# A sparse-softmax attention and low-rank mixer kernel: a planner's order of tasks and PSUM banks replaced by a written-out list, and sixteen loads moved from GpSimd's queue to SyncE's

## The chip, the cores and the metric

The kernel runs on one NeuronCore of one Trainium2 chip. A core has five engines that take their instructions in program order and wait for each other by semaphores: TensorE (PE, matmul and transpose), VectorE (DVE), ScalarE (ACT), GpSimd (POOL) and SyncE (SP, which here only issues DMAs). PE writes into PSUM, which has eight banks of 128 x 512 fp32. The metric is the device time of one launch in microseconds. Before the change four runs gave 603.37, 605.27, 605.30 and 608.26, with a median of 605.28.

## The reference, cut to what matters

```python
batch, n_heads, seq, head_dim = (8, 8, 576, 64)      # tau = 0.02
def _attn_ref(q, k, v, tau):
    scores = (1.0 / np.sqrt(64)) * np.matmul(q, k.transpose(0, 1, 3, 2))
    thresh = np.max(scores, axis=-1, keepdims=True) - tau
    scores = np.where(scores >= thresh, scores, -1000000000.0)
    scores = scores - np.max(scores, axis=-1, keepdims=True)
    attn = np.exp(scores)
    attn = attn / (np.sum(attn, axis=-1, keepdims=True) + 1e-09)
    return np.matmul(attn, v).astype(np.float32)
def _moe_ref(x, U, V, w_ch1, w_ch2):                 # x: heads side by side, (8, 576, 512)
    h = x.transpose(0, 2, 1) @ U @ V                 # rank 32 over the sequence
    u = x + h.transpose(0, 2, 1)
    ch = np.maximum(u @ w_ch1, 0.0) @ w_ch2          # 512 -> 2048 -> 512
    return (u + ch).astype(np.float32)
```

## The kernel before

Two heads form a head pair; there are four pairs in a batch and 32 in all, numbered from 0. A pair has 576 rows, cut into four tiles of 128 and one of 64; the 64-row tiles of two pairs are computed together, so that two pairs need nine score steps, and the whole kernel has 144.

The work of a pair is cut into tasks, each a short Python function that emits a few instructions for one engine. In the order of the data they are: load_tasks (eight DMAs for q and k, L458, and three for v, L480), turn_main and turn_rest (PE transposes q and k, L518 and L531; ACT copies them to SBUF), high, low4 and low (v split into two bf16 halves, ACT L546 and POOL L553), scores (PE, L587, fp32, 16 short matmuls for each step), weigh (DVE, L616, scales the scores and takes the row maximum while it moves them out of PSUM), threshold and exponential (ACT, L632 and L639), select (DVE, L646, keeps what passes the threshold and sums it), twin (POOL, L664, copies a 64-column remainder), turn_w (SP, L670, a DMA that transposes the weights) or turn_pe (PE, L677, the same by TensorE, used for some tiles of the first eight pairs), product (PE, weights times v, L746 to L754), low_part, join and norm (ACT, DVE, POOL: division by the sum), narrow, low_rank, copy_tt, spread and sum_u (the low-rank part), and narrow_u with send_u or turn_u (the transpose of u). A batch then has sixteen up tasks (PE, L930, each four matmuls of 128 x 512), four rest tasks in every second batch (L946), ACT's relu (L920), four or five groups of four down tasks (PE, L963), finish (DVE, L975) and send (SP, L986 and L987). The up and down tasks are the only large blocks of PE work that no later task of the attention waits for.

Every weigh needs its scores in PSUM. A scores task for two steps uses the six banks of the two trio tiles; a task for one step uses four of them. All other PE tasks take one bank each, from those that are free at that time.

The tasks are made in a plain order, and class Order decides in what order they are emitted. Its run is a list scheduler: for each engine it keeps the tasks whose inputs are ready, estimates when each could start from costs written at the tasks, and takes the one with the lowest rank, which is the time at which it became ready plus an offset from the table OFF (one number for each kind of task and phase). The up and down tasks are ranked by DUE and a count of score steps instead. The bank of a task is chosen at the same time. When the estimate leaves PE idle for more than 0.45 us, run emits fillers, which are matmuls of the identity into a free bank (L421, fill) that keep PE busy and whose result nobody reads. What run emits is a fixed program: on the chip each engine executes its list in order.

In the first pairs the queue of an engine matters: a DMA is issued by an engine as an instruction in its list. Pair 0's q and k are loaded by SP, ACT and POOL; those of all later pairs by POOL (variables eq, ek and e3 in load_tasks), v by SP. The mixer's weights are loaded by POOL (weight_loads, L1003 to L1026), spread over the first 30 score steps.

Of the kernel before, what the change touches and what calls it, by code (L numbers as in the profile page):

```python
# [68 lines left out]
P = 128  # L69
# [18 lines left out]
LONE = 2  # L88

# [4 lines left out]
DUE = (461, 86.25, 1468.5, 516.25, 1049.25, 748, 134.75, 1357.5)  # L94
# [32 lines left out]

class Order:


    SIGNAL = (0.25, 0.08, 0.08, 0.08, 0.1)
    LAG = (0.0, 0.07, 0.1, 0.06, 0.0)
    SLOW = (1.0,) * 5
    TO_PE = 0.15
    SELF = 0.07
    WARM = 7.2
    BEFORE = 0.45
    PATIENCE = (0, 0.2, 0.1, 0.9, 1.35)


    BEGIN = (3.34, 4.5, 0.7, 1.3, 0.7)
    LANES = 8
    SHARE = (0.6, 0.4)
    LANDING = (3.1, 1.4)
    SWITCH = {"quadrants": 0.17, None: 0.13}
    PARTS = {"S": "quadrants"}

    HOLD = (61.76, 61.61, 6.12, 44, 94.32, 94.08, 76.76, 0.01, 9.57)
    KEPT = ((), (0, 1, 3, 4), (0, 1, 2, 3, 4, 5))


    OFF = {
        "copy_main": (25.53, 63.74, -194.99, 34.77, -69.14, 17.14, -324, 37.67, -35.45),
        "copy_rest": (6.5, -40.06, -14.53, 24.12, -4.13, -20.91, -46.23, 54.32, -95.65),
        "copy_tt": (-16.03, -64.1, 20.85, -110.66, 55.87, 62.18, -42.53, -53.37, -25.08),
        "copy_u": (89.47, -53.33, 162.09, -74.19, 7.13, 9.51, -102.11, -20.31, -73.82),
        "copy_u4": (-5.3, -56.82, -16.18, -6.54, 49.93, -37.52, 64.79, -22.2, -18.99),
        "copy_w": (75.7, -4.79, -22.58, 20.52, -4.75, 68.84, -1.46, 27.15, 10.06),
        "down": (52.39, 32.35, 33.69, 38.82, 7.25, -27.49, 1.69, 19.34, 131.97),
        "exponential": (61.02, 15.66, 97.71, -26.58, 23.56, 95.43, 116.8, 90.08, 11.21),  # L160
        "finish": (-53.17, -45.71, 51.42, 30.79, -14.22, -26.29, 28.78, 16.33, -75.01),
        "first": (-56.79, 75.89, 0.92, -55.7, 35.86, -3.48, 9.68, 53.63, 1.2),
        "high": (-129.72, -35.78, 31.87, -6.58, 48.08, -20.33, -28.95, -46.46, 84.01),
        "inverse": (46.71, -32.89, 54.08, 22.1, 122.91, 38.13, 143.23, 39.39, -23.27),
        "join": (2.19, 36.38, 69.81, -65.72, -28.72, -7.68, -26.75, 24.75, -3.5),
        "load": (14.89, -38.6, -1.87, -55.09, 439, 169.52, 202.43, 266.17, -64.61),
        "low": (23.82, 3.88, -45.02, 6.6, -28.12, -60.17, -87.19, -43.1, 26.46),
        "low4": (64.5, 130.96, 545.14, -26.82, 13.94, -59.21, 35.95, 265.72, -23.85),
        "low_part": (30.38, 13.98, -26.01, -41.71, 130.31, 109.34, -20.82, -133.07, -1.88),
        "low_rank": (-57.69, 16.1, -2.98, 31.4, -60.74, 41.37, 38.61, 8.08, -35.05),  # L170
        "make": (-18.31, -192.85, -81.78, -52.29, 6.69, -18.25, 12.16, -35.09, 27.21),
        "narrow": (5.95, 39.32, -9.64, -6.72, 1.46, 29.45, -10.31, 45.69, -47.12),
        "narrow_u": (-45.99, -94.08, -136.7, -16.38, -46.01, -113.33, 15.29, 42.82, -0.02),
        "narrow_u4": (2.02, -41.08, 15.16, 12.95, 69.79, 35.67, -44.1, -54.14, 56.42),
        "norm": (60.22, 26.73, 14.75, 16.35, 28.89, -20.28, -16.45, 55.02, 19.4),
        "product": (-38.14, -97.33, -17.17, 18.14, -78.98, 56.88, 40.12, 68.18, -110.66),
        "relu": (44.72, -2.34, -31.3, -83.46, 20.06, -116.77, 10.32, 4.5, -36.91),
        "rest": (64.49, 74.43, 34.29, 18.04, -20.78, -41.41, -55.22, -17.62, 44.45),
        "scores": (-2.16, -56.15, 42.01, -69.96, -15.23, -44.76, 4.79, -16.69, -3.93),
        "select": (-41.99, 29.22, -2.51, 135.03, 570.07, 400.28, 184.53, 231.57, 188.34),  # L180
        "send": (43.87, 17.75, 5.67, -19.7, -14.51, -9.84, 285.3, 70.92, -48.56),
        "send_u": (54.83, -57.33, -16.36, 177.37, 12.48, 121.89, 19.74, 60.45, 25.84),
        "spread": (-216.88, 63.66, -12.54, -9.53, -23.32, -1.29, -122.3, 43.34, 63.38),
        "spread4": (12.62, -19.59, -18, 54.22, -34.85, 61.33, -24.98, -50.63, -66.91),
        "spread_v": (-113.69, -64.83, 6.03, 44.27, 73.51, -47.79, -27.38, 65.24, 2.79),
        "sum_u": (-64.77, 3.32, 13.18, 117.53, -78.44, -9.21, 87.33, 127.21, -64.36),
        "sum_u4": (-96.51, 65.77, 2.32, 38.3, 44.64, 21.12, -125.78, 37.98, 23.47),
        "sums": (195.64, 23.57, 47.14, -31.56, 10.32, -16.1, 35.4, 4.49, -58.98),
        "threshold": (-37.94, -91.24, -43.1, -296.86, 94.89, 36.19, 66.3, 1.07, 12.5),
        "turn4": (-36.19, -43.45, 5.14, 7.01, 54.44, -61.28, 52.57, 29.57, -92.54),  # L190
        "turn_main": (0.34, 20.57, 26.79, -161.06, 126.25, -30.36, -38.23, -14.86, -5.97),
        "turn_pe": (-0.48, -21.65, -184.33, 36.36, -95.83, 51.55, 181.65, 20.16, -43.63),
        "turn_rest": (-5.99, -37.64, -0.75, 52.43, -6.2, -61.13, -8.69, -94.49, -32.06),
        "turn_u": (-85.8, -3, -69.47, -45.79, 74.76, -7.02, 3.37, 12.83, 72.77),
        "turn_w": (45.6, -1.19, -137.3, 47.86, -48.09, 10.25, -28.07, -30.73, 72.41),
        "twin": (32.78, -132.71, -13.72, -15.07, -38.22, -14.87, -64, 49.79, 55.76),
        "up": (13.07, 75.42, -49.49, -57.58, 68.34, -48.43, 10.3, 58.82, 35),
        "values": (-37.57, -25.94, -48.38, 20.3, -54.04, 26.74, 72.56, -4.07, -32.49),
        "weigh": (-145.66, -20.29, -57.18, 79.45, -16.94, 55.31, 45.2, 33.27, 31.94),
        "weights": (-56.28, 79.24, -10.97, 18.21, -35.76, 31.57, -73.46, 67.52, 113.68),  # L200
    }
# [4 lines left out]
    def add(self, *args, **kw):  # L206
        t = Task(*args, **kw)
        t.phase = self.phase
        t.lag = 0.0 if t.dma else self.LAG[t.engine]
        t.off = self.OFF[t.fn.__name__][self.phase]  # L210
        self.tasks.append(t)
        return t

    def run(self):
        ready = [[] for _ in range(5)]
        for t in self.tasks:
            t.left = len(t.deps)
            for d in t.deps:
                d.after.append(t)
            if not t.left:  # L220
                ready[t.engine].append(t)
        at = list(self.BEGIN)
        last = [0.0] * self.nbanks
        kind = None
        steps = 0
        locked = 0.0

        moved = [0.0, 0.0]

        lanes = [0.0] * self.LANES  # L230

        def rank(c):
            s, t = c
            if t.when is not None:
                due = t.when <= steps + (1.0 if t.kind == kind else 0.0)
                return (t.when - 1000.0 if due else t.when + 1000000.0, s)
            return (t.ready + t.off, s)

        left = len(self.tasks)
        while left:  # L240
            best = None
            free = sorted(range(self.nbanks), key=lambda n: last[n])
            kept = self.KEPT[max([t.trios for t in ready[PE] if t.ready <= at[PE] + self.HOLD[t.phase]],
                                 default=0)]
            pool = [n for n in range(self.nbanks) if n not in kept]
            soonest = min(last[n] for n in pool)
            for e in range(5):
                cands = []
                for t in ready[e]:
                    s = max(at[e], t.ready)  # L250
                    if t.banks:
                        s = max(s, soonest)
                    if t.trios:
                        s = max([s] + [last[n] - self.BEFORE * (t.steps == 1)
                                       for n in self.KEPT[t.trios]])
                    if e == POOL and t.dma:
                        s = max(s, lanes[t.ndma - 1 - self.LANES])
                    if s < NEVER:
                        cands.append((s, t))
                if not cands:  # L260
                    continue
                first = min(s for s, _ in cands)
                s, t = min((c for c in cands if c[0] <= first + self.PATIENCE[e]), key=rank)
                if best is None or s < best[0]:
                    best = (s, t)
# [3 lines left out]
            if e == PE:  # L269
# [7 lines left out]
                if parts != self.PARTS.get(kind):  # L277
                    s += self.SWITCH[parts]
# [820 lines left out]
```

## Time and profile before

The profiled execution took 603.37 us, which is the lowest of the four; its span, from the first instruction to the last, is 601.6 us, so that 1.77 us lie around it.

| | busy us | share of the span | instructions |
|---|---|---|---|
| PE | 584.0 | 97% | 6249 |
| DVE | 522.0 | 87% | 1399 |
| ACT | 458.8 | 76% | 959 |
| POOL | 372.1 | 62% | 596 |

The granted TensorE clock is 1.00 in nearly all of the span. The 84 fillers are counted in PE's busy time with 22.9 us. In the breakdown by DMA queue, the queue that SP issues to carries 66.3 MB in 207,680 packets and POOL's carries 22.8 MB in 14,048.

Two things should be kept in mind with this page. Busy times of neighbouring matmuls and of neighbouring vector instructions overlap, since an instruction's record runs until its last result is written; the distance from one start to the next is shorter than the record. A filler's record is 0.379 us long, for instance, but a row of fillers starts one every 0.217 us. And a filler is busy time in the table but not work.

### The profile page before, as it was taken

How to read it: one execution, taken by the hardware profiler on the slowest of the kernel's cores; microseconds unless marked ns; L12 is line 12 of the kernel's file. 1: busy time of each engine (PE TensorE's matmuls, PEld its weight loads, DVE VectorE, ACT ScalarE, POOL GpSimd, SP SyncE). 2: the span in 40 equal slices, each digit the busy share in tenths (PEclk: the TensorE clock that was granted, in tenths of full speed). 3: DMA queues.
4: the chain of work that ended last, by engine and by line, in shares of the span. 5: the costliest groups of instructions: out<-in, count | busy, mean ns of one | idle time of the engine just before them, and what ended most of it. 6: DMA issues, size and time to landing. Idle time of an engine off the chain costs nothing. (4 is left out here: it accounts for less than half of the span.)

```text
span 601.6 us, 17115 instructions
## 1 busy us (share of the span) xinstructions
PE 584.0 (97%) x6249; PEld 349.3 (58%) x6249; DVE 522.0 (87%) x1399; ACT 458.8 (76%) x959; POOL 372.1 (62%) x596
## 2 busy tenths in 40 slices
PE   7999889999999999999999999999999999999996
PEld 3455665666666556555665556555566666556642
DVE  4889999999999999999988999999999999994101
ACT  5757899998899866896789866897699986784540
POOL 9958587687888864576676665776677633342000
PEclk9999999999999999999999999999999999999999
DMA  7799989958999799988998899887999987667203
GB/s 161 112 179 154 169 138 172 167 115 139 206 181 165 135 187 197 172 152 140 196 167 147 147 189 180 164 161 158 188 165 150 177 156 147 124 95 131 45 1 87
DMA packets 222771, 90.48 MB, mean 150 GB/s; under 512 B 200800, under 2 KB 213040, under 8 KB 222688
## 3 DMA queue, kind: packets, MB, share of 16 engines
q1 hardware_dynamic: 207680, 66.30, 65.7%
q0 software_dynamic: 14048, 22.76, 20.6%
q8 instruction: 49, 0.80, 0.6%
q10 hardware_dynamic: 960, 0.34, 0.2%
q14 instruction: 34, 0.28, 0.2%
HBM read 37.90 MB, written 9.44 MB: 79 GB/s over the span
## 5 line engine op out<-in xcount | busy, mean ns | idle before, releaser
L639 ACT ACTIVATE e_sb<-s_sb,m 128x576 bf16<-128x576 f32 x288 | 217.7, 775 | 42.8 <-DVE s_sb L616 33.0
L646 DVE SCALAR_TENSOR_TENSOR w_ring<-s_sb,thr,e_sb 128x576 bf16<-128x576 f32 x288 | 238.7, 858 | 8.8 <-ACT e_sb L639 3.9
L616 DVE TENSOR_SCALAR_CACHE_REDUCE s_sb<-trio 128x576 f32<-128x576 f32 x288 | 203.2, 751 | 16.1 <-PE trio L587 14.9
L587 PE MATMUL trio<-qkT 64*64 64x288 f32 (+2 forms) x2304 | 162.9, 410 | 0.5 <-DVE x L791 0.4
L664 POOL COPY w_ring<-w_ring 128x128 bf16<-128x128 bf16 (+1 forms) x168 | 72.5, 442 | 103.7 <-DVE w_ring L646 82.4
L587 PEld LDWEIGHTS trio<-qkT 64*64 64x64 f32 x2304 | 83.6, 132 | 56.9 <-issue 10.9
L458 POOL DMA_DIRECT2D qkraw<-in_q_dram x125 | 82.3, 663 | 25.1 <-PE bank L518 20.1
L798 POOL TENSOR_TENSOR x<-x,rec 128x256 f32<-128x256 f32 (+1 forms) x84 | 69.5, 830 | 37.4 <-DVE x L791 29.0
L963 PE MATMUL bank<-W2b,R 128*128 128x512 bf16 x368 | 90.2, 379 | 0.4 <-ACT qkT L524 0.3
L963 PEld LDWEIGHTS <-R 128*128 128x128 bf16 x576 | 53.8, 98 | 54.1 <-issue 1.5
L458 POOL DMA_DIRECT2D qkraw<-in_k_dram x125 | 81.3, 658 | 3.0 <-issue 2.2
L930 PE MATMUL bank<-uT,W1b 128*128 128x512 bf16 x320 | 77.8, 379 | 0.7 <-ACT R L920 0.4
L930 PEld LDWEIGHTS <-W1b 128*128 128x128 bf16 x512 | 47.1, 98 | 53.6 <-issue 5.7
L553 POOL TENSOR_TENSOR vh<-vraw_ring,vh 64x128 bf16<-64x128 f32 x64 | 56.1, 877 | 13.8 <-ACT vh L546 8.1
L750 PEld LDWEIGHTS <-wT_ring 128*128 128x128 bf16 x896 | 56.0, 98 | 7.6 <-issue 2.6
L920 ACT ACTIVATE R<-bank 128x512 bf16<-128x512 f32 x91 | 52.7, 595 | 4.8 <-PE bank L930 3.0
L930 PE MATMUL trio<-uT,W1b 128*128 128x512 bf16 x192 | 48.3, 379 | 0.4 <-DVE s_sb L616 0.2
L963 PE MATMUL trio<-W2b,R 128*128 128x512 bf16 x208 | 47.5, 379 | 0.0
L632 ACT ACTIVATE thr<-m,tau_t 128x2 f32<-128x2 f32 x144 | 42.0, 294 | 3.7 <-DVE s_sb L616 3.5
L750 PE MATMUL bank<-vh,wT_ring 128*128 128x128 bf16 x624 | 44.5, 219 | 0.0
L975 DVE TENSOR_TENSOR o<-bank,x 128x512 f32<-128x512 f32 x23 | 15.8, 688 | 32.1 <-PE bank L963 31.9
L746 PE MATMUL bank<-vh,wT_ring 128*128 128x64 bf16 x176 | 33.9, 193 | 0.0
(105 smaller groups left out, 719.7 us busy)
## 6 DMA issues: line engine op xcount, KB each, us to landing
out_dram<-o SPq DMA_DIRECT2D x71, 128.0 KB, 3.1
vraw_ring<-in_v_dram SPq DMA_DIRECT2D x32, 160.0 KB, 3.7
qkraw<-in_k_dram POOLq DMA_DIRECT2D x63, 80.0 KB, 4.4
qkraw<-in_q_dram POOLq DMA_DIRECT2D x62, 80.0 KB, 4.2
vraw_ring<-in_v_dram SPq DMA_DIRECT2D x32, 128.0 KB, 3.9
qkraw<-in_q_dram POOLq DMA_DIRECT2D x63, 64.0 KB, 3.8
qkraw<-in_k_dram POOLq DMA_DIRECT2D x62, 64.0 KB, 4.4
W1b<-in_moe_w_ch_dram POOLq DMA_DIRECT2D x8, 256.0 KB, 6.1
```

The lines of the kernel that those rows point to most:

```text
L458: queue.dma_start(pr.qkraw[part, to, j, :], src[:, j, of, :])
L553: nc.gpsimd.tensor_tensor(out=pr.vh[part, tiles_, :, h, :], in0=raw[part, tiles_], in1=pr.vh[part, tiles_, :, 0, :], op=ALU.subtract)
L587: mm = nc.tensor.matmul(cols[part, lo:hi], a.tT[hs, 0, rows], a.tT[hs, 1, lo:hi], start=True, stop=True)
L616: nc.vector.tensor_scalar(out=s_sb, in0=score_cols(slot, x), scalar1=-scale, scalar2=None, op0=ALU.mult, op1=ALU.min, accum_out=m[:, x:x + 1])
L639: nc.scalar.activation(out=e_sb, in_=s_sb, func=ACT.Exp, bias=m[:, x:x + 1], scale=-1.0)
L646: nc.vector.scalar_tensor_tensor(out=w_sb[:, 0:S], in0=s_sb, scalar=thr_[:, x:x + 1], in1=e_sb, op0=ALU.is_le, op1=ALU.mult, accum_out=pr. ...
L664: nc.gpsimd.tensor_copy(out=w_sb[:, xs, S:640], in_=w_sb[:, xs, 512:S])
L750: nc.tensor.matmul(av[:, 2 * a + j, :], w, pr.vh[:, kt, j, :, :], start=kt == 0, stop=False)
L798: nc.gpsimd.tensor_tensor(out=x, in0=x, in1=over_sum(part), op=ALU.mult)
L920: nc.scalar.activation(out=R2[:, fts, lo:hi], in_=bank[t.got[0]].rearrange("p (f c) -> p f c", c=hi - lo), func=ACT.Relu)
L930: nc.tensor.matmul(bank[t.got[0]], W1b[:, dt, ft * P:(ft + 1) * P], bt.uT[:, dt, :], start=(dt == 0), stop=(dt == 3))
L963: nc.tensor.matmul(ch, R2[:, ft, lo:lo + P], W2b[:, ft, :], start=(ft == 0), stop=(ft == 15))
```

## The change

The scheduler is removed: the tables OFF, HOLD and PATIENCE, the cost constants and the whole selection in run are gone. In its place stand two constants. ORDER lists all 3284 tasks by number in the order in which they are emitted, with negative entries for fillers (-1 - bank); BANK gives the PSUM bank of each task that needs one. The tasks themselves are made in the same order as before, so a number means the same task in both kernels. The list has 56 fillers where the scheduler had emitted 84. It changes the order on all five engines.

The q and k loads of pairs 1 and 2 (counted from 0), eight DMAs each, are issued by SP and no longer by POOL (LOADERS). Two dependencies are added: the second weigh of a two-step scores task is put behind the first (both are on DVE), and the transpose of u of every pair waits for the up tasks of the batch two before it, where only the first pair of a batch did. Some cost numbers at the tasks change, which nothing reads any more, and an unused variant (take and over, for p < ACTED with ACTED = 0) is added.

```diff
+LOADERS = (None, "SSSS", "SSSS")
+ACTED = 0
+ORDER = (
+    23, 21, 22, 25, 20, 26, 24, 19, 44, 28, 46, 40, 27, 29, 42, -1, -1, -1, -1, -1, -1, -1, -1, -1, 32, 41, 30, 33,
...
+)
+BANK = {n: b for b, tasks in {
+    0: (
...
+}.items() for n in tasks}
     def run(self):
-        ready = [[] for _ in range(5)]
...
-            s, t = best
...
+        for n in ORDER:
+            if n < 0:
+                self.filler(-1 - n)
+                continue
+            t = self.tasks[n]
+            assert all(d.end for d in t.deps), "a task before what it needs"
             if t.trios:
                 t.got = list(self.KEPT[t.trios])
             elif t.banks:
-                t.got = [min((n for n in pool if last[n] <= max(s, soonest)),
-                             key=lambda n: (n < 6, n % 3 < 2, last[n]))]
...
+                t.got = [BANK[n]]
             t.fn(t)
...
+            t.end = True
...
-        eq, ek, e3 = (POOL, POOL, POOL) if p else (SP, SCA, POOL)
+        by = {"S": SP, "A": SCA, "P": POOL}
+        eq, ek, eq3, ek3 = (SP, SCA, POOL, POOL) if p == 0 else \
+            (by[c] for c in (LOADERS[p] if p < len(LOADERS) else "PPPP"))
...
-            t = add(VEC, 0.678, weigh, [S_, got("w", tiles[0] + x - NS)],
+            t = add(VEC, 0.678, weigh, [S_, got("w", tiles[0] + x - NS)] + ([done["P1", n - 1, x]] if slot else []),
...
-        deps = [ub] + (done.get(("p1", pr.b - 2), []) if pr.hp == 0 else [])
+        deps = [ub] + done.get(("p1", pr.b - 2), [])
```

## The prediction

> **What bounds the kernel now.** I read the table of busy times first, then the busy times in six stretches (cut at 25, 50, 94, 330 and 532 us), then the same stretches for the fillers' line alone.
>
> ```profile
> PE 584.0 (97%) x6249; PEld 349.3 (58%) x6249; DVE 522.0 (87%) x1399; ACT 458.8 (76%) x959; POOL 372.1 (62%) x596
> ```
>
> ```profile
> 0.00:25.00 25.00, 21.52 (x158) 10.44 (x159) 16.09 (x50) 14.58 (x29) 23.51 (x43) 1.00 0.67 136
> 25.00:50.00 25.00, 23.36 (x320) 14.23 (x317) 20.36 (x59) 15.95 (x32) 18.47 (x36) 1.00 1.18 170
> 50.00:94.00 44.00, 38.95 (x580) 25.83 (x582) 42.23 (x119) 39.36 (x80) 30.99 (x53) 1.00 1.02 158
> 94.00:330.00 236.00, 234.58 (x2602) 144.59 (x2603) 223.68 (x604) 198.74 (x425) 169.43 (x268) 1.00 0.95 164
> 330.00:532.00 202.00, 200.90 (x2147) 119.81 (x2146) 197.33 (x525) 160.25 (x340) 121.50 (x187) 1.00 0.92 160
> 532.00:601.60 69.60, 64.66 (x453) 34.37 (x452) 22.34 (x50) 29.92 (x59) 8.24 (x13) 1.00 0.36 69
> ```
>
> ```profile
> 0.00:25.00 25.00, 10.48 (x35) 3.59 (x36) 1.00 0.67 136
> 25.00:50.00 25.00, 8.78 (x37) 3.14 (x34) 1.00 1.18 170
> 50.00:94.00 44.00, 3.29 (x13) 1.19 (x13) 1.00 1.02 158
> ```
>
> The columns are the stretch, its length, busy PE, PEld, DVE, ACT and POOL, granted clock, DMA share and GB/s; in the second fence PE and PEld are the fillers alone. From 94 us on PE is full (234.58 of 236, 200.90 of 202). Before that up and down have nothing to work on, and a good part of PE's busy time is filler. So the time is PE's own work plus what PE loses, and nearly all of the loss lies in the first 94 us, where the attention's chain and DVE set the pace.
>
> **The ledger.** From the PE timeline I take each kind of task by its usual distance from one start to the next where nothing waits, in us. 128 up and 144 down at 0.864: 235.0. 24 one-step scores at 1.133, 60 two-step at 2.102, and 0.093 for each of 84 changes into scores: 161.1. The products, 56 at 1.009, 28 at 0.505, 8 at 1.05 and 4 at 0.524: 81.1. 64 turn_main at 0.437, 32 turn_rest at 0.110: 31.5. The small ones (rest, low_rank, spread, turn_pe, turn_u, spread4, turn4): 41.8. Sum 550.5, the same in both kernels. The span of 601.6 thus has a loss of 51.1: 36.8 up to score step 25 (PE starts it at 93.9 us with 57.1 of work done), 9.0 from there to step 142 (532.0 us, 486.2 done), 5.3 after it, of which 4.7 follow the last matmul. Up to step 25 the loss is 3.3 before the first instruction, 83 fillers at 0.217 = 18.0, 1.8 because the first nine take 0.42 each, and 13.7 of waits.
>
> DVE gets the same ledger, by the same distances: weigh 0.678, select 0.738, sum_u and finish 0.603, join 0.31, make 0.29, inverse 0.335. The built programs give the order, so the work ahead of a step can be counted in both:
>
> | step | PE starts it, before | PE work ahead, before / after | fillers | DVE work ahead, before / after |
> |---|---|---|---|---|
> | 8 | 35.4 | 14.7 / 14.7 | 53 / 31 | 20.4 / 21.7 |
> | 25 | 93.9 | 57.1 / 58.8 | 83 / 56 | 76.4 / 77.2 |
> | 90 | 339.0 | 297.2 / 285.2 | 84 / 56 | 297.3 / 297.2 |
> | 142 | 532.0 | 486.2 / 479.8 | 84 / 56 | 475.5 / 475.2 |
>
> Two things follow. 27 of the 28 missing fillers are missing before step 25, 22 of them before step 8. And after step 25 the new order brings the scores forward and leaves up and down for later: 12 us at step 90, 6.4 at step 142.
>
> **The moved loads.** These rows are POOL's, SP's, PE's and DVE's timelines:
>
> ```profile
> 3.08 2.62 POOL L458 DMA_DIRECT2D qkraw<-in_q_dram  x4
> 24.78 1.38 POOL L664 COPY w_ring<-w_ring 128x128 bf16<-128x128 bf16 x7
> ```
>
> ```profile
> 3.17 4.36 SPq L480 DMA_DIRECT2D vraw_ring<-in_v_dram  x6
> 25.17 5.14 SPq L670 DMA_TRANSPOSE wT_ring<-w_ring  x3
> ```
>
> ```profile
> 29.23 3.63 PE L421 MATMUL trio<-identb 128*128 128x512 bf16 x16
> 34.80 0.41 PE L754 MATMUL bank<-vh,wT_ring 128*128 128x64 bf16 x8 [1.32 <-DMA wT_ring<-w_ring]
> ```
>
> ```profile
> 32.76 0.82 DVE L646 SCALAR_TENSOR_TENSOR w_ring<-s_sb,thr,e_sb 128x576 bf16<-128x576 f32 x1 [2.85 <-DMA wT_ring<-w_ring]
> ```
>
> Before, POOL issues loads at 0.655 each until 24.78, and the first seven twins stand behind them although DVE's first selects ended by 16 us. So SP's first transpose starts at 25.17, the first product waits behind 16 fillers, and DVE stands 2.85 us for a ring slot. In the new program four tasks of v's split and loads, one weight DMA and pair 0's loads are ahead of the first twin: v lands near 11, ACT's cast 0.7, low4 and low 1.9, two loads 1.3, a weight 0.6, twin near 16. SP has 25 DMAs ahead of its first transpose: 0.74, three in 2.38, 22 at 0.727, which gives 19.1. Transposes start 6 us earlier, and the 16 fillers at step 8 are gone from the list.
>
> What the move costs: pair 1's loads, which POOL had issued by 8.3, are now mixed with v on SP; the last starts at 10.4 and lands 3.7 later (the median of SP's q loads), at 14.1. turn_rest of pair 1 ran at 12.88 and now stands ahead of step 2 with both turn_main (0.98 together), so step 2 starts at 15.2 where it was 14.2: a loss of 1.0, taken in full. Pair 2's loads stand ahead of the first transpose in any case and are in the 19.1.
>
> The Trainium skill ("DMA: Bandwidth & Descriptors", Issuing engines are not separate DMA queues) says that spreading DMAs over issuing engines saves only the sequencer's time, usually small beside the transfer; by that the move gives about nothing. Here sixteen issues of 0.655 are 10.5 us in a queue that a transpose waits behind.
>
> **Fillers.** A filler on the list costs 0.217, one that is left out costs nothing only if the task behind it is ready. I take 27 x 0.217 = 5.9 as gained. From below the bound is 0 (PE waits instead). From above it is DVE's: weigh of step 25 cannot start before 10.3 + 77.2 = 87.5, 1.9 after its scores, so PE starts step 25 no earlier than 85.6 and loses at least 85.6 - 58.8 = 26.8, 10.0 less than now. 36.8 - 5.9 + 1.0 = 31.9 lies between.
>
> Against leaving fillers out speaks the Trainium skill ("TensorE: Matmul & The Clock Gate", Part 1): after an idle window of about 3.4 us PE falls to half clock. By it one such gap would cost some 1.7 us more. The trace shows the slow clock only in the first nine fillers (0.42 against 0.217), and no PE gap over 1.7 us after them.
>
> **Step 25 to 142.** The waits there sum to 9.0. Those over 0.15 us (nineteen, such as low_rank to up 0.60, fill to down 0.46) make 5.5, the rest is in small gaps. Most come where PE stands at one task while up or down could run; an order by single tasks can put one in between. Bounds: 3.5 (all nineteen gone) and 9.0 (none); I take the middle, 6.2.
>
> **The other edits.** Bank numbers cost nothing by themselves; a bank taken too early would show as a PE wait, in the range. The weigh dependency is between neighbours on DVE. The u dependency could hold SP, with every transpose behind it, only if up of two batches earlier is late; when batch 3 begins (steps 54 to 57) 36 up tasks are ahead, 32 are needed. The cost numbers are read by nobody.
>
> **Sum.** 550.5 + 31.9 + 6.2 + 5.3 = 593.9 of span; 1.77 around it gives 595.7 on the profiled run's footing; the median lies 1.91 above that run: 597.6.
>
> **The rivals.** That the change does nothing is excluded: the built lists differ on every engine.
>
> *Nothing gained (605 to 607).* PE waits where it filled, and the 9.0 stays: 36.8 + 9.0, with or without the 1.0. For it: fillers only mark time. Against it: the 2.85 us of DVE and the 16 fillers have one cause, POOL's queue, which is removed.
>
> *DVE becomes the bound (slower, 611).* The new order needs DVE to run ahead. From its first weigh at 10.3 to weigh of step 142 at 534.3 DVE does 475.5 in 524.0, 90.7%. If it does no better, that weigh stays at 534, its scores at 532, and PE still has 70.7 instead of 64.3 to do: 532 + 70.7 + 5.3 = 608.0, or 611.7 as a median. It decides below 475.2 / 517.6 = 91.8%, where the time is as before; my sum needs 93%. For it: from 94 to 330 us the DMA share is 0.95 and transposes must come faster too. Against it: DVE's idle time here is PE's making, since PE is full.
>
> *More gained (591).* DVE's limit is nearly reached in the start (loss 28) and the nineteen waits go: 550.5 + 28 + 3.5 + 5.3 = 587.3, median 591.0.
>
> **Numbers.** Forecast 0.50, more 0.20, nothing 0.16, slower 0.14. A measurement of this kernel tells about 0.5%, that is 3.0 us: faster is below 602.3. Forecast and more are faster: 0.70; same 0.16; slower 0.14. The forecast's own range is 593 to 602 (waits 3.5 to 9.0, the gain in fillers between 5.9 and 3, the 1.0 gone or doubled). For 8 in 10 I take 590 to 606, which leaves out slower and a little below.
>
> **What would show it.** Right: SP's first transpose near 19 us, no wait of select for wT near 30, step 25 started near 90.7, step 142 near 518, DVE at 93% between. Wrong: PE waits of several us in the first 90 us; selects waiting for transposes or weigh for scores after 94 us; a last matmul later than 594.

## The result, and the profile after

The changed kernel takes 604.83 us as a median of 53 runs (600.2 to 611.94), the kernel before 606.21 of 79 (601.34 to 610.24). The ratio is 0.9976, with an interval of 0.9961 to 0.9990. That is a gain of 0.24%, clear of the noise and below the 0.5% that the prediction set as a bound: by its classes, the same. The profiled run took 603.87 us with a span of 602.1, which is 0.5 more than the span of the kernel before; the forecast for it was 593.9.

The first view is again the table of busy times.

```profile
PE 577.9 (96%) x6221; PEld 345.5 (57%) x6221; DVE 515.3 (86%) x1399; ACT 458.3 (76%) x959; POOL 335.7 (56%) x580
```

PE has 6.1 us less busy time, about what the 28 missing fillers took (the fillers' records sum to 22.9 us before and 16.5 after), and yet the span is not shorter. The six stretches (columns as in the prediction) tell where it went:

```profile
0.00:25.00 25.00, 21.40 (x167) 10.78 (x171) 16.74 (x52) 14.05 (x27) 15.06 (x31) 1.00 0.79 155
25.00:50.00 25.00, 22.65 (x342) 14.18 (x342) 24.93 (x73) 20.70 (x43) 20.49 (x38) 1.00 1.11 158
50.00:94.00 44.00, 40.08 (x577) 26.09 (x576) 41.49 (x116) 39.85 (x82) 30.39 (x53) 1.00 1.01 155
94.00:330.00 236.00, 228.82 (x2584) 140.85 (x2582) 226.40 (x612) 196.62 (x419) 155.48 (x266) 1.00 0.96 164
330.00:532.00 202.00, 201.19 (x2144) 120.18 (x2143) 190.88 (x521) 162.85 (x346) 107.24 (x184) 1.00 0.95 157
532.00:601.60 69.60, 63.78 (x420) 33.39 (x417) 14.86 (x30) 24.18 (x49) 7.03 (x11) 0.99 0.39 76
```

From 25 to 50 us DVE is busy for 24.93 of 25 us where it was 20.36: the start is better, as forecast. From 94 to 330 us PE is busy for 228.82 of 236 us where it was 234.58: PE waits 6 us more there, in a stretch where it had been full. The ledger of the prediction, with the same work of 550.5 in both, gives the loss in three parts:

| loss in us | up to step 25 | steps 25 to 142 | behind step 142 | sum | span |
|---|---|---|---|---|---|
| before | 36.8 | 9.0 | 5.3 | 51.1 | 601.6 |
| forecast | 31.9 | 6.2 | 5.3 | 43.4 | 593.9 |
| after | 30.8 | 14.0 | 6.7 | 51.5 | 602.1 |

So 6.0 us were gained up to step 25 and 6.4 given back behind it. PE's timeline names the larger waits (in brackets the idle time before the instruction and what ended it):

```profile
109.71 0.66 PE L572 MATMUL bank<-ident,qkraw 128*128 128x128 f32 x4 [1.70 <-DVE x L859]
...
178.19 0.30 PE L585 MATMUL bank<-ident,qkraw 128*128 128x128 f32 x1 [1.31 <-DMA qkraw<-in_q_dram]
...
233.35 1.02 PE L1031 MATMUL bank<-W2b,R 128*128 128x512 bf16 x4 [1.91 <-DVE o L1043]
...
297.63 0.33 PE L585 MATMUL trio<-ident,qkraw 128*128 128x128 f32 x1 [0.69 <-DVE s_sb L670]
298.30 0.40 PE L964 MATMUL bank<-identb,ub 128*128 128x128 bf16 x4 [0.34 <-ACT ub L957]
...
579.84 1.02 PE L1031 MATMUL trio<-W2b,R 128*128 128x512 bf16 x4 [1.17 <-ACT R L988]
```

(The ledger counts 0.1 to 0.2 more for each, since it goes by the distance of starts.) In the rows of 109.71, 233.35 and 297.63 PE waits for a bank that DVE frees, and DVE's timeline shows why it was late:

```profile
107.01 0.82 DVE L700 SCALAR_TENSOR_TENSOR w_ring<-s_sb,thr,e_sb 128x576 bf16<-128x576 f32 x1 [2.12 <-DMA wT_ring<-w_ring]
...
229.88 2.69 DVE L700 SCALAR_TENSOR_TENSOR w_ring<-s_sb,thr,e_sb 128x576 bf16<-128x576 f32 x1
...
232.61 0.69 DVE L1043 TENSOR_TENSOR o<-bank,x 128x512 f32<-128x512 f32 x1
...
294.37 2.30 DVE L700 SCALAR_TENSOR_TENSOR w_ring<-s_sb,thr,e_sb 128x576 bf16<-128x576 f32 x1
```

At 107 us a select waits 2.12 for a transpose of its ring slot; two more selects and the join (L859) that frees PE's bank stand behind it. At 229.88 a select lasts 2.69 instead of 0.82, and the finish (L1043) that frees PE's bank stands behind it; at 294.37 it is 2.30. POOL's timeline beside the two:

```profile
230.22 0.62 POOL L866 TENSOR_TENSOR x<-x,rec 128x256 f32<-128x256 f32 x1
230.79 1.16 POOL L607 TENSOR_TENSOR vh<-vraw_ring,vh 128x512 bf16<-128x512 f32 x1
...
294.88 1.17 POOL L607 TENSOR_TENSOR vh<-vraw_ring,vh 128x512 bf16<-128x512 f32 x1
```

The low task of pair 13 (L607) runs from 230.79 to 231.95, right behind a norm task (L866), and the select ends 0.62 later. The same holds at 294.37, without a norm: low ends at 296.05, the select at 296.67.

The marks of the start stand as forecast, on SP and on POOL:

```profile
19.12 3.24 SPq L724 DMA_TRANSPOSE wT_ring<-w_ring  x2
```

```profile
15.35 0.30 POOL L718 COPY w_ring<-w_ring 128x128 bf16<-128x128 bf16 x1
```

SP's first transpose is issued at 19.12 (25.17 before; 19.1 forecast), the first twin runs at 15.35 (24.78 before; near 16 forecast), and no select waits for a transpose near 30 us. The later mark does not stand: PE starts step 142 at 524.6, where 518 was forecast.

### The profile page after: what moved, and what is told of

Read it like the earlier page. It is cut to its first block, busy times and chain, and to the rows that moved or that the text cites. A ratio compares the mean times of both kernels' runs of the same rounds, so it can differ in the third digit from the quotient of the medians.

```text
span 602.1 us, 16997 instructions
## 1 busy us (share of the span) xinstructions
PE 577.9 (96%) x6221; PEld 345.5 (57%) x6221; DVE 515.3 (86%) x1399; ACT 458.3 (76%) x959; POOL 335.7 (56%) x580
## 4 chain that ended last, share of the span: by engine, by line
PE 55%; DVE 19%; DMA 6%; issue 5%; ACT 5%; SPq 1%; POOL 0%; DVEq 0%; ACTq 0%; POOLq 0%
PE trio L641 13%; DVE w_ring L700 9%; PE trio L998 8%; PE bank L998 6%; PE trio L1031 6%; PE bank L1031 6%; DVE s_sb L670 6%; DMA wT_ring<-w_ring 4%; PE bank L804 4%; PE trio L804 3%; ACT e_sb L693 2%; PE bank L572 1%; DVE o L1043 1%; PE trio L572 1%; DMA qkraw<-in_q_dram 1%
## 5 line engine op out<-in xcount | busy, mean ns | idle before, releaser
L693 ACT ACTIVATE e_sb<-s_sb,m 128x576 bf16<-128x576 f32 x288 | 215.8, 774 | 39.9 <-DVE w_ring L700 27.4
L718 POOL COPY w_ring<-w_ring 128x128 bf16<-128x128 bf16 (+1 forms) x168 | 66.9, 404 | 127.3 <-DVE w_ring L700 92.3
L510 POOL DMA_DIRECT2D qkraw<-in_q_dram x117 | 76.7, 657 | 12.2 <-PE bank L572 4.9
L866 POOL TENSOR_TENSOR x<-x,rec 128x256 f32<-128x256 f32 (+1 forms) x84 | 54.9, 660 | 38.6 <-DVE x L859 25.0
L607 POOL TENSOR_TENSOR vh<-vraw_ring,vh 64x128 bf16<-64x128 f32 (+1 forms) x64 | 53.9, 842 | 23.7 <-ACT vh L600 11.1
L998 PE MATMUL trio<-uT,W1b 128*128 128x512 bf16 x272 | 65.6, 379 | 0.4 <-ACT tt L885 0.4
L998 PE MATMUL bank<-uT,W1b 128*128 128x512 bf16 x240 | 59.5, 379 | 0.0
L988 ACT ACTIVATE R<-trio 128x512 bf16<-128x512 f32 x74 | 41.8, 597 | 15.6 <-PE trio L998 13.5
L988 ACT ACTIVATE R<-bank 128x512 bf16<-128x512 f32 x70 | 40.7, 595 | 5.3 <-PE bank L1014 3.3
L804 PE MATMUL bank<-vh,wT_ring 128*128 128x128 bf16 x512 | 36.7, 219 | 0.0
L1043 DVE TENSOR_TENSOR o<-trio,x 128x512 f32<-128x512 f32 x13 | 8.9, 690 | 31.5 <-PE trio L1031 31.4
```

What stands on the lines that cost most here:

```text
L510: queue.dma_start(pr.qkraw[part, to, j, :], src[:, j, of, :])
L607: nc.gpsimd.tensor_tensor(out=pr.vh[part, tiles_, :, h, :], in0=raw[part, tiles_], in1=pr.vh[part, tiles_, :, 0, :], op=ALU.subtract)
L693: nc.scalar.activation(out=e_sb, in_=s_sb, func=ACT.Exp, bias=m[:, x:x + 1], scale=-1.0)
L718: nc.gpsimd.tensor_copy(out=w_sb[:, xs, S:640], in_=w_sb[:, xs, 512:S])
L804: nc.tensor.matmul(av[:, 2 * a + j, :], w, pr.vh[:, kt, j, :, :], start=kt == 0, stop=False)
L866: nc.gpsimd.tensor_tensor(out=x, in0=x, in1=over_sum(part), op=ALU.mult)
```

## The experiments

All ratios are to the kernel before, run on the same chip; the parts of the loss are from each kernel's profiled run. "DVE idle" is the time up to the weigh of step 142 less DVE's work ahead of it, by the prediction's ledger.

| run | ratio | interval | up to 25 | 25 to 142 | behind 142 | sum | DVE idle |
|---|---|---|---|---|---|---|---|
| before | 1 | | 36.8 | 9.0 | 5.3 | 51.1 | 58.8 |
| after | 0.9976 | 0.9961 to 0.9990 | 30.8 | 14.0 | 6.7 | 51.5 | 51.0 |
| new start, old list | 0.9878 | 0.9824 to 0.9932 | 31.2 | 8.7 | 5.1 | 45.0 | 52.9 |
| old start, new list | 1.0102 | 1.0053 to 1.0152 | 37.8 | 19.2 | 6.5 | 63.5 | 63.2 |
| loads back on POOL | 0.9969 | 0.9936 to 1.0001 | 31.1 | 16.1 | 6.6 | 53.8 | 53.5 |
| loads moved alone | 1.0013 | 0.9978 to 1.0049 | 39.9 | 8.8 | 5.2 | 53.9 | 61.7 |
| five places on PE and DVE | 0.9978 | 0.9948 to 1.0007 | 28.8 | 15.5 | 5.0 | 49.3 | 50.5 |
| two low tasks | 0.9960 | 0.9931 to 0.9988 | 30.6 | 12.5 | 6.8 | 49.9 | 49.4 |
| old list, 35 fillers fewer | 1.0042 | 1.0008 to 1.0076 | 41.0 | 9.2 | 5.2 | 55.4 | 63.1 |
| new start, 12 fillers | 0.9942 | 0.9914 to 0.9970 | 33.8 | 9.8 | 5.2 | 48.7 | 56.3 |
| old list, 25 fillers fewer | 1.0032 | 1.0003 to 1.0062 | 39.4 | 12.0 | 5.2 | 56.6 | 64.3 |
| low tasks and tail | 0.9896 | 0.9850 to 0.9941 | 29.0 | 13.5 | 4.9 | 47.4 | 48.7 |
| low, tail and v loads | 0.9859 | 0.9825 to 0.9892 | 30.6 | 7.4 | 5.0 | 43.0 | 44.3 |
| v loads alone | 0.9982 | 0.9949 to 1.0015 | 30.6 | 12.8 | 6.8 | 50.2 | 49.7 |

One caution for the column "up to 25": six kernels have the changed kernel's list and loads unchanged up to step 25, and lie between 28.8 and 30.8. A difference of 2 us in one profile of the start is no finding.

A second one concerns PE's granted clock. In every profile it is 1.00 from 6 to 10 us on, but for the last few microseconds and, in some, stretches of 3.41 or 6.83 us at 0.50. Between steps 25 and 142 there are such stretches in "old start, new list" (two, from 199.6 and from 244.0 us), "loads back on POOL" (from 112.2), "five places" (109.6), "two low tasks" (110.7) and "old list, 25 fillers fewer" (110.4), and none in the other rows. One of 3.41 us can make up 1.7 us of that column (an estimate: half its length).

**Was the gain of the start given back by the list behind it?** The first run has the new list up to score step 23 and everything else in the old order, the second the reverse (with the loads on POOL).

```diff
-ORDER, BANK = new
+ORDER, BANK = new up to the scores of step 23, then the rest in the old order
```

> The new list up to score step 23, the old order and banks for everything after it. Theory 'given back': the new list gains some 6 us of PE loss before step 25 (36.8 to 30.8 in the traces) and loses it after that by waits that belong to the later part of the list (9.0 to 14.0, and 5.3 to 7.3 behind step 142). Then the loss here is 30.8 + 9.0 + 5.3 and the span about 596, a ratio of 0.990. Rival 'elastic': whatever is gained early is lost later, because transposes and DVE cannot keep up with an earlier start in any order; then the loss between steps 25 and 142 grows to 13 or more here too and the ratio is 0.997 to 1.000.

```diff
-ORDER, BANK = new
+ORDER, BANK = old up to the scores of step 23, then the rest in the new order
-LOADERS = (None, "SSSS", "SSSS")
+LOADERS = ()
```

> The old order (loads of pairs 1 and 2 on POOL) up to score step 23, the new list and banks after it. Theory 'given back': loss 36.8 + 14.0 + 7.3, a span near 608.6, ratio 1.010. Rival 'elastic': the later part loses less when it starts later, about 9 and 5, span near 602, ratio 1.000.

The first came out at 0.9878, the second at 1.0102, near what the theory of "given back" says. In the first the losses are where it puts them, 31.2 and then 8.7. In the second they are 37.8 and then 19.2, which is 5.2 more than the theory's 14.0; the two stretches of slow clock can be 3.4 of these, and the profiled execution was the slowest of its six. The new list behind step 25 is worse than the old one after either start. The elastic rival falls, since an early start keeps its gain with the old list behind it. The first run is faster than both kernels.

**Which part of the change makes the start faster?**

```diff
-LOADERS = (None, "SSSS", "SSSS")
+LOADERS = ()
```

> The changed kernel with the q and k loads of pairs 1 and 2 back on POOL, everything else in the same list. If the move is what makes the start faster: the first twin comes again behind some 20 us of POOL's loads, SP's first transpose near 25 us, the loss at step 25 rises from 30.8 to 35 or more, ratio 1.005 to 1.010 against the kernel before. If the order does it and the move nothing: first transpose below 21 us or loss at step 25 below 32, ratio as the changed kernel's, 0.998.

```diff
-ORDER, BANK = new
+ORDER, BANK = old
 LOADERS = (None, "SSSS", "SSSS")
```

> The old order and banks, with the q and k loads of pairs 1 and 2 issued by SP: the move alone. The 83 fillers ahead of step 25 stay on the list, 18.0 us. If the move frees the start: first transpose near 19 us, DVE's 2.85 us wait at 30 us gone, loss at step 25 33 to 35 in place of 36.8, ratio 0.994 to 0.997. If a list made for late transposes cannot use it: loss 36 to 38, ratio 0.999 to 1.003.

The list does it, not the move. With the loads back on POOL the start loses 31.1; with the move alone 39.9, which is 3.1 more than before and more than either expectation said (its time can't be told from that of the kernel before). SP's first transpose in the one and in the other, POOL's first twin in the first, and a load of POOL's in the second:

```profile
17.54 4.19 SPq L664 DMA_TRANSPOSE wT_ring<-w_ring  x2
```

```profile
27.50 5.01 SPq L664 DMA_TRANSPOSE wT_ring<-w_ring  x3
```

```profile
17.19 0.32 POOL L658 COPY w_ring<-w_ring 128x128 bf16<-128x128 bf16 x1
```

```profile
16.35 2.62 POOL L450 DMA_DIRECT2D qkraw<-in_q_dram  x4 [12.13 <-PE bank L525]
```

In the new list the first twin stands behind two of the eight loads of pair 3, but ahead of the other six, of the loads of Ub and of four casts of Vb. So the transpose is early even when the sixteen loads are put back into POOL's queue, where all of them stand ahead of that twin. In the old list seven twins stand behind all eight loads of pair 3, and taking the sixteen loads out of the queue doesn't bring the twins forward: POOL stands 12.13 us at the first load of pair 3, which waits for PE to free its buffer, and the twins come at 26.65. No run moved the twins alone, so that their place is what makes the start faster is argued from these times. The move alone makes step 2 start at 17.1 instead of 14.2, since pair 1's loads wait among v's on SP.

**Are the late waits a matter of where PE's and DVE's tasks stand?**

```diff
-DVE: 666 select, 664 select, 678 select, 580 join, 695 weigh
+DVE: 580 join, 666 select, 664 select, 695 weigh, 678 select
-PE: 1288, 1284, 1286 transposes of pair 12, 1033 product, 845 rest
+PE: 1033 product, 845 rest, 1288, 1284, 1286 transposes of pair 12
-DVE: 1386 select, 867 finish
+DVE: 867 finish, 1386 select
-DVE: 1785 select, 1891 weigh, 1890 weigh
+DVE: 1890 weigh, 1785 select, 1891 weigh
-PE: 2870 down, 3250 rest, ... 2871 down, ... 3230 up, 3278 down, 2872 down, 3254 down, 3255 down
+PE: 2870 down, 2871 down, 2872 down, 3250 rest, ... 3230 up, 3254 down, 3255 down, 3278 down
```

Four bank numbers change with the order.

> The changed kernel with its list altered at five places only, where PE waited over 1.3 us after 94 us. DVE's join of pair 4 (it frees the bank that turn_main of pair 8 waits for at 109.7) ahead of two selects that wait for a transpose; a product and a rest task ahead of the transposes of pair 12, whose load lands late (178.2); finish of batch 1's third tile ahead of the select that lasted 2.69 us (233.4); a weigh ahead of the select that lasted 2.30 us (297.6); the last two downs of batch 6 ahead of batch 7's relus, and the first 64-row down behind two others (568 and 580). Fifteen tasks out of 3284 move, four banks change. Theory 'local': each wait is only that place's, the waits shrink by 1.3 + 1.4 + 2.0 + 1.4 + 1.0 = 7.1 us and nothing takes their place: span near 595, loss 44.4, ratio to the kernel before 0.986 (0.983 to 0.989). Rival 'elastic': PE is ahead of DVE and the DMAs, and what it doesn't lose here it loses at the next task that needs them: loss 49 to 51.5, ratio 0.994 to 0.998.

Mostly not: 0.9978. Only the last place is local (5.0 behind step 142 instead of 6.7). Idle times of PE in the profile: near 105 us 0.57, 0.65 and 1.44, two of them for weighs, in place of 1.70 for the join, and behind the last the granted clock is 0.51 from 109.5 to 113 us, which the changed kernel's profile doesn't have; near 180 us 0.68 and 0.41 in place of 1.31; the select at 230.69 still lasts 1.97 and PE waits 1.23 in place of 1.91. Where PE's bank comes free late because DVE is held by a third engine, another order on DVE passed the wait to the next task here. So the next runs touch that third engine.

**POOL's low task and the long selects.**

```diff
-POOL: 1404 norm, 1312 low (pair 13), 1389 twin
+POOL: 1404 norm, 1389 twin, 1312 low (pair 13)
-POOL: 1779 twin, 2077 load, 2081 load, 1721 low (pair 17)
+POOL: 1721 low (pair 17), 1779 twin, 2077 load, 2081 load
```

> The changed kernel with two of POOL's tasks moved in the list and nothing else: the low task of pair 13 from before to behind the twin that waits for the select of 229.88 us, and the low task of pair 17 six POOL tasks earlier. Theory 'the low task held the select': the selects that lasted 2.69 and 2.30 us last 0.8 to 1.0, PE's wait of 1.98 at 233.4 and of 0.85 at 297.6 are gone, the time between steps 25 and 142 loses 14.0 - 2.8 = 11.2, span near 599.3, ratio 0.993 (0.990 to 0.996). Rival 'the select waited for something else that the records don't show' (a DMA, a ring slot): the same two selects still last over 2 us, ratio 0.9976 as in the changed kernel.

The select of the first place, on DVE, and the down behind it, on PE:

```profile
230.37 0.82 DVE L640 SCALAR_TENSOR_TENSOR w_ring<-s_sb,thr,e_sb 128x576 bf16<-128x576 f32 x1
...
231.23 0.69 DVE L983 TENSOR_TENSOR o<-bank,x 128x512 f32<-128x512 f32 x1
```

```profile
231.97 1.02 PE L971 MATMUL bank<-W2b,R 128*128 128x512 bf16 x4
```

The select lasts 0.82 and PE no longer waits; the same at the other place. Two POOL tasks moved by a few microseconds, and the loss from step 64 to 142 is 5.8 instead of 8.0. The ratio of 0.9960 agrees, though its interval and that of the changed kernel overlap, so that the time alone shows no gain. That the low task held the select is shown by the durations, and that these two waits of PE came from it.

**Are fillers time?** The prediction counted 0.217 us for each one left out.

```diff
-ORDER, BANK, LOADERS = new
+ORDER, BANK, LOADERS = old, without 35 of its 84 fillers
```

> The kernel before's list, banks and loads, with 35 of its 84 fillers left out (the 16 at step 8 among them), everything else as it was; 49 fillers are left, fewer than the changed kernel's 56. Theory 'a filler is time': each is worth 0.217 us, the loss up to step 25 falls from 36.8 to 29.2, ratio 0.9875 (0.985 to 0.992). Rival 'fillers only mark time': PE waits where it filled, the loss at step 25 stays 36 to 38, ratio 0.997 to 1.003. If the loss grows instead, an idle PE is slower afterwards: matmuls behind the gaps would take longer than their usual distance.

```diff
-ORDER, BANK = new up to the scores of step 23, then the rest in the old order
+ORDER, BANK = the same, without the 45 fillers behind the first 12
```

> The list of the best version so far (new to step 23, then the old; 0.9878) without the 45 fillers that stand behind the first 12. Theory 'a filler is time': up to 45 x 0.217 = 9.8 us, loss at step 25 near 21 to 22; DVE's own bound of 26.8 allows 4.4 of it, so a ratio near 0.981. Rival 'fillers only mark time': loss at step 25 stays near 31, ratio 0.985 to 0.991. Rival 'fillers keep PE fast': matmuls after the gaps take longer, ratio above 0.992.

```diff
-ORDER = old, without 35 of its 84 fillers
+ORDER = the same, with ten of the sixteen fillers of step 8 put back
```

> The list with 49 fillers (the kernel before's, with 35 left out) with ten of the sixteen fillers of step 8 put back: 59 fillers, 25 fewer than in the kernel before. Without any, PE stood 3.67 us there and the granted clock was 0.50 from 33.7 to 40 us; ten fillers leave a gap of about 1.5 us. Theory 'fillers only hold the clock': no slow matmuls near 35 us, granted clock 1.00 from 25 to 50 us, loss at step 8 back from 21.0 to 20.7 and at step 10 from 24.3 to 22.0, loss at step 25 near 37 to 38 (36.8 in the kernel before), ratio 0.998 to 1.002: 25 fillers fewer are worth nothing and cost nothing. Rival 'a filler is time': ten more than in that run cost 2.2 us, 25 fewer than in the kernel before save 5.4 us. If a second gap over 2.5 us comes near 73 us again, the loss stays 2 us higher.

All three lose against their full lists: 41.0 and 39.4 up to step 25 instead of 36.8, and 33.8 instead of 31.2. In the times the first and the last are slower than the kernel before; the intervals of the second and of its full list overlap. PE's timeline and its windows (length, busy time, granted clock, DMA share, GB/s) of the first:

```profile
33.67 0.61 PE L746 MATMUL bank<-vh,wT_ring 128*128 128x64 bf16 x8 [3.67 <-DMA wT_ring<-w_ring]
...
35.70 2.43 PE L579 MATMUL trio<-qkT 64*64 64x288 f32 x16
```

```profile
30.00:33.70 3.70, 0.03 (x1) 0.93 1.28 165
33.70:35.70 2.00, 2.00 (x37) 0.50 1.16 222
35.70:38.00 2.30, 2.30 (x18) 0.50 1.19 205
38.00:40.00 2.00, 2.00 (x12) 0.51 1.62 94
40.00:42.00 2.00, 2.00 (x28) 1.00 1.03 222
```

PE stands for 3.67 us where the sixteen fillers were, and behind that the granted clock is 0.50 until 40 us: a score step takes 2.43 us instead of 1.20, a product's row 0.61 instead of 0.41. The other executions say the same: the granted clock of the whole execution is below 0.993 in 11 of the 12 of this run, and in 1 of the 33 of the kernel before beside it. So these fillers are no time that can be saved, since PE waits for the same transpose without them, and too few cost more than they take. The forecast for the third run was wrong: with ten put back the gap was 1.62, and the clock still fell to 0.50 from 35.3 to 42.1 us. Later in that run a wait of 2.46 for a transpose at 110.7 was followed by a clock of 0.80 and 0.77 (108 to 116 us): steps 25 to 36 took 43.2 us where they took 39.6 in the kernel before, more than the whole of what its 12.0 is above 9.0. In its profiled run the changed kernel with its 56 fillers has a clock of 1.00 in the whole start, and its longest gap there is 1.58. That is no property of the list: the run with the two low tasks has the same list and fillers up to there, and its clock was 0.50 for 3.41 us from 28.7 us, behind a gap of 1.26. Its loss up to step 25 was 30.6 all the same.

**The end, and the v loads.** The next run has the two low tasks and, from the five places, only the last.

```diff
-ORDER = new
+ORDER = new, with the low tasks 1312 and 1721 and the downs 2871, 2872 and 3278 moved as above
```

> The changed kernel with the two low tasks moved as before and, in the last part, the last two downs of batch 6 ahead of batch 7's relus and the first 64-row down behind two others. Theory 'both are local and add up': loss between steps 25 and 142 11 to 12.5 (14.0 in the changed kernel), behind step 142 5.0 (7.3), total loss 47 to 48.5, ratio 0.993 (0.990 to 0.996); the waits of 0.47 and 1.33 at 568 and 580 are gone. Rival 'elastic': what is saved comes back in other waits, total loss 50 to 51.5, ratio 0.996 to 0.999. The best version (0.9878) is not reached by either.

It reached 0.9896, clear of the changed kernel, with a loss of 47.4: 4.9 behind step 142, as "local" says. (Four of the expectations put 7.3 for the changed kernel there; 51.5 less 44.8 at step 142 is 6.7.) But the term from step 25 to 142 is 13.5 and not the 11 to 12.5 of "local"; the total fits because this execution's start lost 29.0, with the same list up to step 25. What remains is the wait near 105 us, which took 5.7 us from step 25 to 36 in this run. There v loads stand between the transposes on SP:

```profile
94.94 1.21 SPq L664 DMA_TRANSPOSE wT_ring<-w_ring  x1
96.20 1.29 SPq L474 DMA_DIRECT2D vraw_ring<-in_v_dram  x2
97.54 3.67 SPq L664 DMA_TRANSPOSE wT_ring<-w_ring  x1
101.26 1.25 SPq L474 DMA_DIRECT2D vraw_ring<-in_v_dram  x2
102.62 2.66 SPq L664 DMA_TRANSPOSE wT_ring<-w_ring  x2
```

```diff
-SP: 546 turn_w, 629 v, 647 v, 539 turn_w, 648 v, 627 v, 571 turn_w, 559 turn_w, 649 v
+SP: 546 turn_w, 539 turn_w, 571 turn_w, 559 turn_w, 629 v, 627 v, 647 v, 648 v, 649 v
```

> The run with the two low tasks and the tail moved (ratio 0.9896, total loss 47.4), and one thing more: on SP four v loads of pairs 6 and 7, which stand between the transposes of pair 5 issued at 94.9, 97.5 and 102.6 us, are moved behind the last of these. What it tests: in the changed kernel's order a select near 105 waits 2.1 to 4.1 us for a transpose of its ring slot (3.85 in that run), two more selects, a join and the bank that turn_main needs stand behind it, and PE loses 2.2 to 5.1 us at score step 32. Theory 'v loads hold the transposes up': the transposes of pair 5 are issued back to back and land 1.5 to 3 us earlier, that select waits under 2 us, PE's loss from step 25 to 36 falls from 5.7 to 3 to 4, total loss 44.5 to 46, ratio 0.986 to 0.988. Rival 'the transfers share the DMA engines and the order on SP changes nothing': the select waits 3 us or more, total loss 47 to 48, ratio 0.989 to 0.991. Against both: v comes too late for the cast near 114 us, and a new wait of 1 to 3 us appears there.

SP's timeline of the run with the v loads behind, and then the DMA issues from 92 to 112 us (the last number is the median time from issue to landing), without and with the move:

```profile
96.48 8.34 SPq L664 DMA_TRANSPOSE wT_ring<-w_ring  x4
104.87 3.25 SPq L474 DMA_DIRECT2D vraw_ring<-in_v_dram  x5
```

```profile
wT_ring<-w_ring SPq DMA_TRANSPOSE x4, 8.1
```

```profile
wT_ring<-w_ring SPq DMA_TRANSPOSE x6, 5.7
```

The transposes land 5.7 us after their issue instead of 8.1, no select waits near 105 us, and the loss from step 25 to 36 is 1.2. Other transfers of the same stretch landed sooner too (the loads of W2b 5.3 us after issue instead of 7.6), so that not all of the difference need come from the order on SP. The ratio is 0.9859, the best of all, with a span of 593.5: the list of the changed kernel with twelve of its 3284 tasks elsewhere reaches what the prediction forecast for the list as it was. Against the new start with the old list (0.9878) it is not told apart by the times.

```diff
-ORDER = new
+ORDER = new, with only the four v loads moved
```

> The changed kernel with nothing but the four v loads of pairs 6 and 7 moved behind the transposes of pair 5 on SP. The run before had this together with the low tasks and the tail: total loss 43.0, of it 1.2 from step 25 to 36 (3.4 in the changed kernel). Theory 'the places are independent': the select near 105 does not wait, the loss from step 25 to 36 is 1 to 1.5, from 36 to 142 it stays at the changed kernel's 10 to 11, the tail at 7.3, total loss 48.5 to 50, ratio 0.991 to 0.995. Rival 'only together' (what is saved at 105 us is lost again at the two long selects and in the last part): total loss 50.5 to 52, ratio 0.996 to 0.999.

Alone, the v loads gave 0.9982, which can't be told from the changed kernel. In the profile the two long selects are back and the losses behind step 36 as well (9.8, 10.6 in the changed kernel), as "independent" says; but the select near 105 us waited 1.66 and the loss from step 25 to 36 was 3.0, not 1 to 1.5. In the changed kernel and three other runs with its order there that select waited 2.12 to 4.13, in the two with the v loads moved 0 and 1.66. The direction is shown; how much of the 0.9859 this edit brought is open, since the times of the runs with and without it overlap.

## Why the prediction was wrong

**PE's work.** The 550.5 us are the same tasks in every list; all losses here are taken against them, so the runs are no test of this term.

**The start: right in size, wrong in its cause.** Forecast 31.9, measured 30.8; step 25 at 89.6, forecast 90.7. But the working put it down to the moved loads and to 27 fillers of 0.217. The move is worth nothing: the loss is 31.1 without it in the new list and 39.9 with it in the old. What the prediction saw in POOL's queue was right (twins behind loads, SP's transpose behind the twins), but it took the sixteen moved loads for the cause. POOL's timeline up to 24.78 also holds the eight loads of pair 3, which can't start before PE frees their buffer (at 16.35 in the run with the move alone), the mixer's loads and 2.2 us of casts, and the twins stay behind those when the sixteen are gone. What the runs leave as the remedy is the twins' place in the list. The move's cost for pair 1's loads, taken as 1.0, was 2.9 in the old list at step 2 and nothing in the new one (step 2 at 13.6). And "a filler on the list costs 0.217" is refuted for these lists by the filler runs: leaving fillers out didn't gain in any of the three. That 27 x 0.217 = 5.9 comes close to the 6.0 gained is luck: both lists wait for transposes, the new one gets them earlier, and so fewer fillers stand ahead of them. For a gap that is left unfilled the prediction estimated 1.7 us from the skill's rule; in the old list without the fillers of step 8 steps 8 to 10 lost 3.3 instead of 1.3.

**Steps 25 to 142: the step that failed.** The prediction took "the middle, 6.2" between 3.5 (all nineteen waits gone) and 9.0 (none gone), and it was 14.0. It reckoned with a new order that takes waits away and adds none, so the upper bound held only the old list's waits. A new order drops those and makes its own, and nothing in the old list bounds these. The larger ones are a select behind a transpose near 105 us, two selects behind low tasks on POOL, and a late load at 178 us (1.38, which wasn't mended alone). With the first three mended (and the tail) the term is 7.4, near the forecast, and the ratio 0.9859: the list had the gain that the prediction expected of it, and three places ate it. Shown is this for the three together; the two low tasks alone and the v loads alone are not told from the changed kernel by their times.

**Behind step 142.** Forecast 5.3, measured 6.7: two downs of batch 6 that the new list keeps among batch 7's ups wait for relus (0.31 and 1.17 of idle time in the profile). Moved ahead, 4.9.

**The sum.** 8.2 us of span too short: 7.8 from the middle, 1.4 from the end, less 1.1 at the start.

**The rivals.** "Nothing gained" came nearest to the time (605 to 607, measured 604.83), but not for its reasons: the start did gain 6.0, and the 9.0 did not stay. "DVE becomes the bound" was nearer the mechanism than its 0.14 said: up to the weigh of step 142 DVE does 475.2 us of work in 516.4, 92.0%, just beyond the 91.8% from which it was to decide and short of the 93% of the sum. What kept DVE from more was in good part transposes and POOL, not the DVE work itself: in the best run its idle time is 6.7 us less than in the changed kernel.

## What to carry to other kernels

A loss term for a changed order has no upper bound in the old order's waits: leave its range open upwards, and look for the three or four places where an engine one step removed (a transposing queue, POOL beside DVE) holds the one that frees the banks. Here such a wait was mended at the engine that caused it; moving the waiting tasks on DVE passed it on. And filler on PE is counted as time only if the task behind it is ready.

## What the runs showed of the hardware

A select on DVE (two inputs in SBUF) lasts 0.81 to 0.82 us alone. Where a low task on POOL had begun before it, it ended 0.61 us or more after the low task, in all 158 such pairs of the fourteen profiles (those in which only one task of POOL's with two inputs met the select), and in 126 of them not later than 0.63. The Trainium skill ("SBUF — State Buffer", Who interferes with whom) says that a DVE instruction with two SBUF inputs contends with a GpSimd one that reads SBUF, and that the order of issue decides who blocks. Most rows agree: where the select began first, it could keep its 0.81 while the low task was drawn out (in the kernel before, at 385.71, to 1.78 us instead of 1.16). The two rows of the result don't: with low beginning 0.51 us after the select, and a norm 0.34 and low 0.91 us after it, the select lasted 2.30 and 2.69 us, so the one that came second went first. Why is open; with the low task moved, a norm again 0.34 us behind the select was the one that was drawn out (0.94 us instead of 0.62).

The granted clock fell to 0.50 behind these idle times of PE: 3.67 us (for 6.83 us), 2.71 and 2.62 us (for 3.41 each), 1.62 us behind ten fillers (6.83), and 1.26 us in the run with the two low tasks (3.41). It did not fall behind 1.28 us at the same place of the changed kernel's profile, behind 1.91 us at 233 us there, nor behind 3.14 us in the run with low tasks and tail (107.1 to 110.2 us). So the length of a gap alone does not decide. The Trainium skill ("TensorE: Matmul & The Clock Gate", What's actually happening) gives a free-running window of about 3.4 us, and one idle window as the cause. The lengths of 3.41 and 6.83 us agree with such a window; the falls behind 1.62 and 1.26 us show that PE need not stand for a whole one. The clock differs from execution to execution as well: of the changed kernel's 53 runs, the 13 with a granted clock of 0.998 or more have a median of 601.5 us, the 11 below 0.993 one of 608.0.
